# Halving the first batch's attention so that the feed-forward can start earlier

## The chip, the cores and the metric

The kernel runs on one core of a Trainium2 chip. The time is device microseconds of one execution; a figure for a kernel is the median of its runs.

Engines in the profile: PE is the tensor engine's matmuls, PEld its weight loads, DVE the vector engine, ACT the scalar engine, POOL the GpSimd engine, SP the engine that here issues the DMA transposes and the output DMAs. A name such as `po` stands for a tile of the program.

## The reference

Sorted block attention over 4 batches, 8 heads, 768 tokens of 64 values, then a bilinear feed-forward (FFN) over all 3072 tokens.

```python
# q, k, v: (4, 8, 768, 64); sort_net: (4, 8, 8, 8); 8 blocks of 96 tokens
for _ in range(5):                       # P: 8 x 8 per head
    P = exp(P - max(P));  P /= P.sum(-1);  P /= P.sum(-2)
k_sorted = einsum('bhij,bhjcd->bhicd', P, k_b)     # each new block mixes ALL blocks of k
v_sorted = einsum('bhij,bhjcd->bhicd', P, v_b)
scores = scale * q_b @ k_sb.T                      # only inside one block
x = softmax(scores) @ v_sb                         # -> (3072, 512)
out = ((x @ w_a) * (x @ w_b)) @ w_out              # 512 -> 1536 -> 512
```

Sorted k and v need all the tokens of a head, but from the scores on, each block of 96 tokens stands alone. So does each token in the FFN.

## The kernel before

The work is cut into 16 groups `g` of two heads (a "pair"), four pairs to a batch. A batch's FFN needs the x of its four pairs. The kernel does batch 0's attention alone (the "head" of the kernel) and then runs the FFN of batch b with the attention of batch b+1 interleaved. The PE order is fixed by the program; the other engines are ordered by a scheduler. `t` below is one of two halves of a batch's tokens, `m` one of 12 slices of the FFN width.

```python
def to_xT(g, pool, tag):                  # attention result -> transposed x
    xT = xT_of(g // HP)
    nc.sync.dma_start_transpose(out=_ap(xT, ...), in_=st[g, "xp"]...)

def ffn_ab(b, m, t, pool):
    # for w_a, then w_b: four matmuls of 384 columns into pf;
    # ACT copies the first to a_sb, then
    nc.vector.tensor_mul(out=hT[:, m, t * HW:(t + 1) * HW], in0=a_sb, in1=ab[1][:, 0:HW])

def ffn_out(b, c, pool):                  # 128 rows of the output, six times a batch
    po = pool.tile([P, DMODEL], FP32, tag="F", name="po")
    for m in range(KO):
        nc.tensor.matmul(po, lhsT=hT[:, m, c * P:(c + 1) * P], rhs=w_out_sb[:, m, :], ...)
    o_sb = ffp.tile([P, DMODEL], FP32, tag="o_sb", name="o_sb", bufs=3)
    # ACT or DVE copies po to o_sb
    rows = out[b * S:(b + 1) * S, :].rearrange("(p c) n -> c p n", c=NCH)
    nc.sync.dma_start(out=rows[c], in_=o_sb)          # 128 rows, 6 apart
...
for g in range(1, HP):
    stage_q(g, ps0b, "B")                 # q transposes of all four pairs come first
C0(0); C0(1); R0(0); O0(0); to_xT(0, ps0b, "B")       # C: mix, R: scores and v, O: output
C0(2); R0(1); O0(1); to_xT(1, ps0b, "B")
C0(3); R0(2); O0(2); to_xT(2, ps0b, "B")
R0(3); O0(3); to_xT(3, ps0b, "B")
```

The softmax here doesn't subtract the row's maximum and nothing guards it: scores larger than these inputs give would overflow.

## Time and profile before

| | before |
|---|---|
| time, median | 275.3 us at first, 275.81 us over the 4 runs scored with the change |
| span of the profile | 274.4 us |
| PE busy | 238.8 us (87%) |
| first complete FFN (all four matmuls of a group past their waits) | 47.8 us |
| first output matmul (`po`) of batches 0 to 3 | 91.5, 149.2, 207.0, 254.2 us |

The page shows two rows of 40 slices of 6.9 us: the clock granted to PE in tenths, and the mean busy share of the 16 DMA engines in tenths.

```profile
PEclk9999965699999999999999999999999999999999
...
DMA  6999999999993642010110321101011330000132
```

The clock falls to about half in slices 6 to 8 (34 to 55 us).

The next lines are from the page's chain of waits by engine, and from its list of DMAs: count, size of one, median time from issue to landing.

```profile
PE 85%; DMA 7%; POOL 3%; DVE 3%; issue 1%; ACT 0%; POOLq 0%; DVEq 0%; ACTq 0%
...
out_dram<-o_sb SPq DMA_DIRECT2D x24, 256.0 KB, 2.0
...
xT<-xp SPq DMA_TRANSPOSE x16, 2.9
```

PE is 85% of the chain. The same chain in order of time (start, duration, what) shows the head and the first two starts of the output matmuls:

```profile
9.52 8.01 DMA q_102<-in_q_dram
...
17.57 0.85 PE q_ps L131 x9
18.42 2.56 PE mix L145 x40
...
36.64 11.07 DMA xT<-xp
...
47.76 1.76 PE pf L228 x5
...
91.50 0.21 PE po L244
...
149.23 0.22 PE po L244
```

The first mix stands behind the q transposes, and these behind the load that landed at 17.5 us. Later, PE stands behind four DMA transposes of x, one for each pair; the last of them took 11.07 us from issue to landing. From 47.76 us on, everything in this chain up to the last output copy is PE, and a batch takes 57.7 us (149.23 - 91.50).

### The profile page before, as it was taken

Reading aid. Unit: us, or ns where it says so; the run is one execution under the profiler, and the core shown is the slowest. Engines: PE = TensorE matmul, PEld = TensorE weight load, DVE = VectorE, ACT = ScalarE, POOL = GpSimd, SP = SyncE. Lnnn points to the kernel's source line nnn. Section 1 sums busy time; section 2 is a strip of 40 time slices with the busy share of each in tenths; the row PEclk is TensorE's granted clock in tenths of the full one; section 3 lists DMA queues with packets and bytes.
Section 4 is the critical chain, followed back from the end, with each engine's and each line's share of the span. In section 5 each row is a group of like instructions: output and inputs, shape, how many; then the busy total and the mean of one; then the engine's idle time right before and its main releaser. Section 6 shows DMA issues by size and latency. Waiting matters only on the chain.

```text
span 274.4 us, 5477 instructions
## 1 busy us (share of the span) xinstructions
PE 238.8 (87%) x2272; PEld 144.2 (53%) x2280; DVE 122.5 (45%) x268; ACT 98.5 (36%) x194; POOL 48.7 (18%) x67
## 2 busy tenths in 40 slices
PE   0257621999999999999999999999999999999993
PEld 0255510666666545666666446676665455566441
DVE  5836720355555412556554315556644224444111
ACT  2027600446364301644635115354552024333110
POOL 8863349835432000000000000000000000000000
PEclk9999965699999999999999999999999999999999
DMA  6999999999993642010110321101011330000132
GB/s 88 187 202 203 183 183 193 177 185 179 183 176 62 108 122 107 10 29 7 25 31 2 105 102 54 30 2 31 0 32 38 109 113 0 0 2 0 38 117 78
DMA packets 35193, 23.96 MB, mean 87 GB/s; under 512 B 14176, under 2 KB 32096, under 8 KB 35168
## 3 DMA queue, kind: packets, MB, share of 16 engines
q0 software_dynamic: 18864, 14.16, 35.5%
q1 hardware_dynamic: 16304, 9.45, 13.9%
q8 instruction: 18, 0.29, 0.5%
q14 instruction: 7, 0.06, 0.1%
HBM read 28.32 MB, written 6.29 MB: 126 GB/s over the span
## 4 chain that ended last, share of the span: by engine, by line
PE 85%; DMA 7%; POOL 3%; DVE 3%; issue 1%; ACT 0%; POOLq 0%; DVEq 0%; ACTq 0%
PE pf L228 46%; PE po L244 23%; PE mix L145 4%; DMA xT<-xp 4%; PE vs_ps L177 3%; PE o_ps L189 3%; DMA q_102<-in_q_dram 3%; PE sc L166 3%; PE q_ps L131 2%; DVE xp L196 1%; DVE vs_115 L179 1%; DVE rec L193 0%; ACT kT_106 L155 0%; POOL k_77 L78 0%; POOL v_88 L78 0%
## 5 line engine op out<-in xcount | busy, mean ns | idle before, releaser
L228 PE MATMUL pf<-xT,w_a_sb 128*128 128x384 bf16 x384 | 79.9, 330 | 11.3 <-DMA xT<-xp 9.6
L237 DVE TENSOR_TENSOR hT<-a_sb,pf 128x384 bf16<-128x384 bf16 x96 | 53.1, 553 | 78.1 <-PE pf L228 67.9
L228 PE MATMUL pf<-xT,w_b_sb 128*128 128x384 bf16 x384 | 78.8, 328 | 0.0
L236 ACT CAST a_sb<-pf 128x384 bf16<-128x384 f32 x96 | 46.0, 479 | 82.8 <-PE pf L228 51.6
L244 PE MATMUL po<-w_out_sb,hT 128*128 128x512 bf16 x280 | 62.9, 379 | 0.4
L228 PEld LDWEIGHTS <-w_b_sb 128*128 128x128 bf16 x384 | 37.8, 99 | 29.5 <-DMA k_236<-in_k_dram 4.1
L228 PEld LDWEIGHTS <-w_a_sb 128*128 128x128 bf16 x384 | 35.5, 98 | 30.4 <-issue 7.1
L244 PEld LDWEIGHTS <-hT 128*128 128x128 bf16 x288 | 28.0, 98 | 32.8
L250 DVE COPY o_sb<-po 128x512 f32<-128x512 f32 x12 | 8.3, 692 | 43.9 <-PE po L244 43.9
L248 ACT COPY o_sb<-po 128x512 f32<-128x512 f32 x12 | 7.0, 585 | 49.2 <-PE po L244 33.9
L196 DVE TENSOR_TENSOR xp<-o_ps,rec 96x512 bf16<-96x512 f32 x32 | 21.2, 684 | 0.5
L135 DVE COPY qT<-q_ps 128x768 bf16<-128x768 bf16 x16 | 8.8, 551 | 3.4 <-PE q_ps L131 3.4
L155 ACT CAST kT_106<-mix 128x384 bf16<-128x384 f32 x12 | 5.2, 482 | 14.3 <-PE mix L145 14.3
L170 ACT ACTIVATE eT_112<-sc 96x768 bf16<-96x768 f32 x12 | 9.1, 802 | 2.0 <-PE sc L166 1.9
L193 DVE RECIPROCAL rec<-o_ps 96x8 f32<-96x8 f32 x32 | 5.2, 185 | 8.7 <-PE o_ps L189 8.7
L170 ACT ACTIVATE eT_113<-sc 96x768 bf16<-96x768 f32 x10 | 7.5, 803 | 1.2 <-PE sc L166 1.2
L170 ACT ACTIVATE eT_114<-sc 96x768 bf16<-96x768 f32 x10 | 7.5, 802 | 0.9 <-PE sc L166 0.9
L131 PE MATMUL q_ps<-ident,q_81 128*64 128x128 bf16 x12 | 0.9, 313 | 7.8 <-DMA q_81<-in_q_dram 7.8
L155 ACT CAST kT_108<-mix 128x384 bf16<-128x384 f32 x10 | 4.3, 482 | 5.3 <-PE mix L145 5.3
L155 ACT CAST kT_107<-mix 128x384 bf16<-128x384 f32 x10 | 4.3, 482 | 5.1 <-PE mix L145 5.1
L258 POOL TENSOR_TENSOR s_all<-mask,p_col 128x1024 bf16<-128x1024 bf16 x3 | 5.9, 2000 | 0.0
L189 PE MATMUL o_ps<-vs_115,eT_112 96*128 96x65 bf16 x96 | 4.0, 193 | 1.6 <-DVE vs_115 L179 1.6
(205 smaller groups left out, 183.4 us busy)
## 6 DMA issues: line engine op xcount, KB each, us to landing
out_dram<-o_sb SPq DMA_DIRECT2D x24, 256.0 KB, 2.0
w_a_sb<-in_moe_w_a_dram POOLq DMA_DIRECT2D x4, 384.0 KB, 11.4
w_b_sb<-in_moe_w_b_dram POOLq DMA_DIRECT2D x4, 384.0 KB, 12.4
w_out_sb<-in_moe_w_out_dram POOLq DMA_DIRECT2D x3, 512.0 KB, 8.6
xT<-xp SPq DMA_TRANSPOSE x16, 2.9
k_77<-in_k_dram POOLq DMA_DIRECT2D x1, 192.0 KB, 3.5
v_79<-in_v_dram POOLq DMA_DIRECT2D x1, 192.0 KB, 4.6
q_81<-in_q_dram POOLq DMA_DIRECT2D x1, 192.0 KB, 4.9
```

What stands on the lines that cost most here:

```text
L135: nc.vector.tensor_copy(out=qT.rearrange("p i c t -> p c i t"), in_=q_ps.rearrange("p c (i t) -> p c i t", i=NB))
L145: nc.tensor.matmul(mix[e * D:(e + 1) * D, c // 3, c % 3 * P:(c % 3 + 1) * P], lhsT=src2[:, e, c * D:(c + 1) * D], rhs=s_all[:, 2 * g + e], ...
L155: nc.scalar.copy(out=d1, in_=s1)
L166: nc.tensor.matmul(sc[:, e, i * BLK:(i + 1) * BLK], lhsT=kT[e * D:(e + 1) * D, blk * BLK:blk * BLK + P], rhs=qT[e * D:(e + 1) * D, blk], s ...
L170: nc.scalar.activation(out=eT[:, hf, :, 0:HB], in_=sc[0:BLK, :, 0:HB], func=AF.Exp, scale=float(scale))
L189: nc.tensor.matmul(o_ps[:, e, i * (D + 1):(i + 1) * (D + 1)], lhsT=eT[:, hf, e, i * BLK:i * BLK + P], rhs=vs[:, hf * NBH + i, e, 0:D + 1], ...
L196: nc.vector.tensor_tensor(out=_ap(xp, hf * NBH * 2 * D, [[NB * 2 * D, BLK], [D, 2], [2 * D, NBH], [1, D]]), in0=_ap(o_ps, 0, [[1024, BLK], ...
L228: nc.tensor.matmul(pf[:, 0:HW], lhsT=w_sb[:, kc, m * P:(m + 1) * P], rhs=_ap(xT, kc * S + t * 3 * CG, [[KA * S, P], [CG, 3], [BLK, NB], [1 ...
L236: nc.scalar.copy(out=a_sb, in_=pf[:, 0:HW])
L237: nc.vector.tensor_mul(out=hT[:, m, t * HW:(t + 1) * HW], in0=a_sb, in1=ab[1][:, 0:HW])
L244: nc.tensor.matmul(po, lhsT=hT[:, m, c * P:(c + 1) * P], rhs=w_out_sb[:, m, :], start=(m == 0), stop=(m == KO - 1))
L250: nc.vector.tensor_copy(out=o_sb, in_=po)
```

## The change

The intent: let batch 0's FFN start when half of its attention is done. For each pair, only blocks 0 to 3 are scored, normalized and transposed (on PE, with a PSUM copy, instead of by DMA) before the FFN of those blocks starts. Blocks 4 to 7 follow, interleaved with the first FFN half; batch 1's attention is then interleaved with the second half. q is loaded by halves, and the first mix no longer waits for all pairs.

For this, an FFN half must be "four blocks" where it had been "three of six token phases". So the product is written regrouped, and the rows that lie in one output tile change. Core of the diff, with cuts marked by dots and the loop of the head shortened partly into words:

```diff
-    load_pair(0, 0) ... for hp in range(1, HP): load_pair(0, hp)
+    for g in range(HP):
+        load_q_half(g, 0)
+        # k, v of the pair
...
+    def to_xT(g, pool, tag, h, eng):
+        xT, xp = xT_of(g // HP), st[g, "xp"]
+        for i in range(n):
+            nc.tensor.matmul(xt_ps[:, i, :], lhsT=xp[:, i0 + i],
+                             rhs=ident[0:BLK, 0:BLK], is_transpose=True)
+        copy(eng, ...xT..., xt_ps...)
...
-        nc.vector.tensor_mul(out=hT[:, m, t * HW:(t + 1) * HW], in0=a_sb, in1=ab[1][:, 0:HW])
+        nc.vector.tensor_tensor(
+            out=_ap(hTs[b], m * S + t * HW,
+                    [[KO * S, P], [CG, NBH], [NBH * CG, NCH], [1, CG]]),
+            in0=..., in1=_ap(pf, 0, [[512, P], [BLK, NBH], [CG, NCH], [1, CG]]), op=ALU.mult)
...
-        rows = out[b * S:(b + 1) * S, :].rearrange("(p c) n -> c p n", c=NCH)
-        nc.sync.dma_start(out=rows[c], in_=o_sb)
+        nc.sync.dma_start(
+            out=_ap(out, (b * S + t * NBH * BLK + 2 * c) * DMODEL,
+                    [[DMODEL, 2], [NCH * DMODEL, NBH * CG], [1, DMODEL]]),
+            in_=o_sb)
...
+            for g in range(HP + 1):        # head: half 0 only
+                if g < HP:  stage_q(g, ..., 0) if g > 1; mix k, first copy
+                if g > 0:   stage_o(g - 1, ps0, "A", 0)
+                if g < HP:  mix v, first copy; stage_scores(g, ps0, "A", 0)
+                if g > 0:   to_xT(g - 1, ps0b, "B", 0, nc.vector)
+                if g < HP:  stage_v(g, ps0b, "B", 0); second copies of k and v
...
+            second = {0: [(Q1, 0)], 1: [(Q1, 1)], 2: [(S1, 0)], 3: [(V1, 0)], ... 17: [(X1, 3)]}
```

More of the change, by code (lines that the diff above doesn't have):

```diff
@@ L81, in load_pair, with load_q_half @@
         loaded[b * HP + hp] = tiles
-    load_pair(0, 0)
-    make_identity(nc, ident, nomemset=True)
-    for hp in range(1, HP):
-        load_pair(0, hp)
+    HPT = P // 2
+    def load_q_half(g, h):
+        q2 = loaded[g][2]
+        nc.gpsimd.dma_start(
+            out=q2[h * HPT:(h + 1) * HPT],
+            in_=_ap(q, 2 * g * S * D + h * HPT * W, [[W, HPT], [S * D, 2], [1, W]]))
+    make_identity(nc, ident, nomemset=True)
+    for g in range(HP):
+        loaded[g] = [ld.tile([P, 2, W], BF16, tag=n, name=n) for n in ("k2", "v2", "q2")]
+        load_q_half(g, 0)
+        for to, t in zip(loaded[g], (k, v)):
+            nc.gpsimd.dma_start(out=to, in_=_ap(t, 2 * g * S * D, [[W, P], [S * D, 2], [1, W]]))
     mask = const.tile([P, CG], BF16, name="mask")
@@ L95 @@
     NBUF = 3
-    kTs = [const.tile([P, S + PAD], BF16, name=f"kT{n}") for n in range(NBUF)]
-    vTs = [const.tile([P, S + PAD], BF16, name=f"vT{n}") for n in range(NBUF)]
+    NKV = 5
+    HK = HB + PAD
+    kTs = [const.tile([P, 2, HK], BF16, name=f"kT{n}") for n in range(NKV)]
+    vTs = [const.tile([P, 2, HK], BF16, name=f"vT{n}") for n in range(NKV)]
     eTs = [const.tile([BLK, 2, 2, HB + PAD], BF16, name=f"eT{n}") for n in range(NBUF)]
@@ L100 @@
     for t in kTs + vTs:
-        nc.vector.memset(t[:, S:], 0.0)
+        nc.vector.memset(t[:, :, HB:], 0.0)
     for t in eTs:
@@ L124, with copy, blocks, stage_q @@
     st = {}
-    def stage_q(g, pool, tag):
+    def copy(eng, out, in_):
+        if eng is nc.scalar:
+            nc.scalar.copy(out=out, in_=in_)
+        else:
+            eng.tensor_copy(out=out, in_=in_)
+    def blocks(h):
+        return (0, NB) if h is None else (h * NBH, NBH)
+    def stage_q(g, pool, tag, eng, h=None):
         q2 = loaded[g][2]
-        q_ps = pool.tile([P, NCH, P], BF16, tag=tag, name="q_ps")
+        i0, n = blocks(h)
+        p0, np_ = i0 * CG, n * CG
+        q_ps = pool.tile([P, NCH, np_], BF16, tag=tag, name="q_ps")
         for c in range(NCH):
@@ L131, in stage_q, with stage_mix @@
                 nc.tensor.matmul(q_ps[e * D:(e + 1) * D, c, :],
-                                 lhsT=q2[:, e, c * D:(c + 1) * D],
-                                 rhs=ident, is_transpose=True)
-        qT = qtp.tile([P, NB, NCH, CG], BF16, tag="qT", name="qT")
-        nc.vector.tensor_copy(out=qT.rearrange("p i c t -> p c i t"),
-                              in_=q_ps.rearrange("p c (i t) -> p c i t", i=NB))
-        st[g, "qT"] = qT
-    def stage_mix(g, what, pool, tag, engines):
+                                 lhsT=q2[p0:p0 + np_, e, c * D:(c + 1) * D],
+                                 rhs=ident[p0:p0 + np_, p0:p0 + np_], is_transpose=True)
+        if (g, "qT") not in st:
+            st[g, "qT"] = qtp.tile([P, NB, NCH, CG], BF16, tag="qT", name="qT")
+        copy(eng, st[g, "qT"][:, i0:i0 + n].rearrange("p i c t -> p c i t"),
+             q_ps.rearrange("p c (i t) -> p c i t", i=n))
+    def stage_mix(g, what, pool, tag):
         src2 = loaded[g][0 if what == "k" else 1]
-        to = (kTs if what == "k" else vTs)[g % NBUF]
         mix = pool.tile([P, 2, 512], FP32, tag=tag, name="mix")
@@ L145, in stage_mix @@
                 nc.tensor.matmul(
-                    mix[e * D:(e + 1) * D, c // 3, c % 3 * P:(c % 3 + 1) * P],
+                    mix[e * D:(e + 1) * D, c // 4, c % 4 * P:(c % 4 + 1) * P],
                     lhsT=src2[:, e, c * D:(c + 1) * D],
                     rhs=s_all[:, 2 * g + e], start=True, stop=True)
-        for hf, eng in enumerate(engines):
-            n = 2 // len(engines)
-            for u in range(n):
-                d1 = _ap(to, (hf + u) * 3 * CG, [[S + PAD, P], [CG, 3], [BLK, NB], [1, CG]])
-                s1 = _ap(mix, (hf + u) * 512, [[1024, P], [P, 3], [CG, NB], [1, CG]])
-                if eng == "act":
-                    nc.scalar.copy(out=d1, in_=s1)
-                else:
-                    nc.vector.tensor_copy(out=d1, in_=s1)
@@ L159, in stage_scores @@
-    def stage_scores(g, pool, tag):
-        kT, qT, eT = kTs[g % NBUF], st[g, "qT"], eTs[g % NBUF]
-        for hf in range(2):
-            sc = pool.tile([P, 2, 512], FP32, tag=tag, name="sc")
-            for i in range(NBH):
-                for e in range(2):
-                    blk = hf * NBH + i
-                    nc.tensor.matmul(
-                        sc[:, e, i * BLK:(i + 1) * BLK],
-                        lhsT=kT[e * D:(e + 1) * D, blk * BLK:blk * BLK + P],
-                        rhs=qT[e * D:(e + 1) * D, blk], start=True, stop=True)
-            nc.scalar.activation(out=eT[:, hf, :, 0:HB], in_=sc[0:BLK, :, 0:HB],
-                                 func=AF.Exp, scale=float(scale))
@@ L173, in stage_v, with evac_mix @@
-    def stage_v(g, pool, tag):
-        vT, vs = vTs[g % NBUF], vss[g % NBUF]
-        vs_ps = pool.tile([P, NB, 2, D], BF16, tag=tag, name="vs_ps")
-        for i in range(NB):
-            nc.tensor.matmul(vs_ps[:, i], lhsT=vT[:, i * BLK:i * BLK + P],
+        st[g, what] = mix
+    def evac_mix(g, what, eng, h=None):
+        mix, to = st[g, what], (kTs if what == "k" else vTs)[g % NKV]
+        for hf in range(2) if h is None else (h,):
+            copy(eng, _ap(to, hf * HK, [[2 * HK, P], [CG, NCH], [BLK, NBH], [1, CG]]),
+                 _ap(mix, hf * NBH * CG, [[1024, P], [P, NCH], [CG, NBH], [1, CG]]))
@@ new lines, in stage_scores @@
+    def stage_scores(g, pool, tag, h):
+        kT, qT, eT = kTs[g % NKV], st[g, "qT"], eTs[g % NBUF]
+        sc = pool.tile([P, 2, 512], FP32, tag=tag, name="sc")
+        for i in range(NBH):
+            for e in range(2):
+                blk = h * NBH + i
+                nc.tensor.matmul(
+                    sc[:, e, i * BLK:(i + 1) * BLK],
+                    lhsT=kT[e * D:(e + 1) * D, h, i * BLK:i * BLK + P],
+                    rhs=qT[e * D:(e + 1) * D, blk], start=True, stop=True)
+        nc.scalar.activation(out=eT[:, h, :, 0:HB], in_=sc[0:BLK, :, 0:HB],
+                             func=AF.Exp, scale=float(scale))
@@ L178, in stage_v @@
+    def stage_v(g, pool, tag, h=None):
+        vT, vs = vTs[g % NKV], vss[g % NBUF]
+        i0, n = blocks(h)
+        vs_ps = pool.tile([P, n, 2, D], BF16, tag=tag, name="vs_ps")
+        for i in range(n):
+            nc.tensor.matmul(vs_ps[:, i], lhsT=vT[:, (i0 + i) // NBH, (i0 + i) % NBH * BLK:(i0 + i) % NBH * BLK + P],
                              rhs=ident, is_transpose=True)
-        nc.vector.tensor_copy(out=vs[:, :, :, 0:D], in_=vs_ps[0:BLK])
-    def stage_o(g, pool, tag):
+        nc.vector.tensor_copy(out=vs[:, i0:i0 + n, :, 0:D], in_=vs_ps[0:BLK])
@@ L182, in stage_o @@
+    def stage_o(g, pool, tag, h):
         eT, vs = eTs[g % NBUF], vss[g % NBUF]
-        xp = att.tile([BLK, NB, 2, D], BF16, tag="xp", name="xp")
-        rec = att.tile([BLK, 2, 2, NBH], FP32, tag="rec", name="rec")
-        for hf in range(2):
-            o_ps = pool.tile([P, 2, 512], FP32, tag=tag, name="o_ps")
-            for i in range(NBH):
-                for e in range(2):
-                    nc.tensor.matmul(o_ps[:, e, i * (D + 1):(i + 1) * (D + 1)],
-                                     lhsT=eT[:, hf, e, i * BLK:i * BLK + P],
-                                     rhs=vs[:, hf * NBH + i, e, 0:D + 1],
-                                     start=True, stop=True)
-            nc.vector.reciprocal(
-                out=rec[:, hf],
-                in_=_ap(o_ps, D, [[1024, BLK], [512, 2], [D + 1, NBH]]))
-            nc.vector.tensor_tensor(
-                out=_ap(xp, hf * NBH * 2 * D, [[NB * 2 * D, BLK], [D, 2],
-                                               [2 * D, NBH], [1, D]]),
-                in0=_ap(o_ps, 0, [[1024, BLK], [512, 2], [D + 1, NBH], [1, D]]),
-                in1=_ap(rec, hf * 2 * NBH, [[4 * NBH, BLK], [NBH, 2], [1, NBH], [0, D]]),
-                op=ALU.mult)
@@ L202, in stage_o @@
-        st[g, "xp"] = xp
+        if (g, "xp") not in st:
+            st[g, "xp"] = att.tile([BLK, NB, 2, D], BF16, tag="xp", name="xp")
+        xp = st[g, "xp"]
+        rec = att.tile([BLK, 2, NBH], FP32, tag="rec", name="rec")
+        o_ps = pool.tile([P, 2, 512], FP32, tag=tag, name="o_ps")
+        for i in range(NBH):
+            for e in range(2):
+                nc.tensor.matmul(o_ps[:, e, i * (D + 1):(i + 1) * (D + 1)],
+                                 lhsT=eT[:, h, e, i * BLK:i * BLK + P],
+                                 rhs=vs[:, h * NBH + i, e, 0:D + 1],
+                                 start=True, stop=True)
@@ L204 @@
+        nc.vector.reciprocal(
+            out=rec, in_=_ap(o_ps, D, [[1024, BLK], [512, 2], [D + 1, NBH]]))
+        nc.vector.tensor_tensor(
+            out=_ap(xp, h * NBH * 2 * D, [[NB * 2 * D, BLK], [D, 2], [2 * D, NBH], [1, D]]),
+            in0=_ap(o_ps, 0, [[1024, BLK], [512, 2], [D + 1, NBH], [1, D]]),
+            in1=_ap(rec, 0, [[2 * NBH, BLK], [NBH, 2], [1, NBH], [0, D]]),
+            op=ALU.mult)
     xTs = {}
@@ L209, in xT_of, with to_xT_dma @@
         return xTs[b]
-    def to_xT(g, pool, tag):
+    def to_xT(g, pool, tag, h, eng):
+        xT, xp = xT_of(g // HP), st[g, "xp"]
+        i0, n = blocks(h)
+        xt_ps = pool.tile([P, n, BLK], BF16, tag=tag, name="xt_ps")
+        for i in range(n):
+            nc.tensor.matmul(xt_ps[:, i, :], lhsT=xp[:, i0 + i],
+                             rhs=ident[0:BLK, 0:BLK], is_transpose=True)
+        copy(eng, _ap(xT, g % HP * S + i0 * BLK, [[KA * S, P], [1, n * BLK]]),
+             xt_ps.rearrange("p i t -> p (i t)"))
+    def to_xT_dma(g):
         xT = xT_of(g // HP)
@@ L218, with ffn_mm, ffn_a @@
     hTs = {}
-    def ffn_ab(b, m, t, pool):
+    def ffn_mm(b, m, t, w_sb, pool):
+        pf = pool.tile([P, 512], FP32, tag="F", name="pf")
+        for kc in range(KA):
+            nc.tensor.matmul(pf[:, 0:HW], lhsT=w_sb[:, kc, m * P:(m + 1) * P],
+                             rhs=xTs[b][:, kc, t * HW:(t + 1) * HW],
+                             start=(kc == 0), stop=(kc == KA - 1))
+        return pf
+    def ffn_a(b, m, t, pool):
+        pf = ffn_mm(b, m, t, w_a_sb, pool)
+        a_sb = ffp.tile([P, HW], BF16, tag="a_sb", name="a_sb", bufs=4)
+        nc.scalar.copy(out=a_sb, in_=pf[:, 0:HW])
+        st[b, m, t] = a_sb
@@ L221, in ffn_ab, with ffn_b @@
+    def ffn_b(b, m, t, pool):
         if b not in hTs:
             hTs[b] = ffp.tile([P, KO, S], BF16, tag="hT", name="hT")
-        hT, xT = hTs[b], xTs[b]
-        ab = []
-        for w_sb in (w_a_sb, w_b_sb):
-            pf = pool.tile([P, 512], FP32, tag="F", name="pf")
-            for kc in range(KA):
-                nc.tensor.matmul(
-                    pf[:, 0:HW], lhsT=w_sb[:, kc, m * P:(m + 1) * P],
-                    rhs=_ap(xT, kc * S + t * 3 * CG,
-                            [[KA * S, P], [CG, 3], [BLK, NB], [1, CG]]),
-                    start=(kc == 0), stop=(kc == KA - 1))
-            ab.append(pf)
-            if len(ab) == 1:
-                a_sb = ffp.tile([P, HW], BF16, tag="a_sb", name="a_sb", bufs=4)
-                nc.scalar.copy(out=a_sb, in_=pf[:, 0:HW])
@@ L237, in ffn_ab @@
-        nc.vector.tensor_mul(out=hT[:, m, t * HW:(t + 1) * HW], in0=a_sb,
-                             in1=ab[1][:, 0:HW])
-    def ffn_out(b, c, pool):
+        pf = ffn_mm(b, m, t, w_b_sb, pool)
+        nc.vector.tensor_tensor(
+            out=_ap(hTs[b], m * S + t * HW,
+                    [[KO * S, P], [CG, NBH], [NBH * CG, NCH], [1, CG]]),
+            in0=st[b, m, t].rearrange("p (i c s) -> p i c s", i=NBH, c=NCH),
+            in1=_ap(pf, 0, [[512, P], [BLK, NBH], [CG, NCH], [1, CG]]),
+            op=ALU.mult)
@@ L241, in ffn_out @@
+    def ffn_out(b, t, c, pool):
         hT = hTs[b]
+        c0 = t * HW + c * P
         po = pool.tile([P, DMODEL], FP32, tag="F", name="po")
         for m in range(KO):
-            nc.tensor.matmul(po, lhsT=hT[:, m, c * P:(c + 1) * P], rhs=w_out_sb[:, m, :],
+            nc.tensor.matmul(po, lhsT=hT[:, m, c0:c0 + P], rhs=w_out_sb[:, m, :],
                              start=(m == 0), stop=(m == KO - 1))
         o_sb = ffp.tile([P, DMODEL], FP32, tag="o_sb", name="o_sb", bufs=3)
-        if c % 2 == 0:
-            nc.scalar.copy(out=o_sb, in_=po)
-        else:
-            nc.vector.tensor_copy(out=o_sb, in_=po)
@@ L251, in ffn_out @@
-        rows = out[b * S:(b + 1) * S, :].rearrange("(p c) n -> c p n", c=NCH)
-        nc.sync.dma_start(out=rows[c], in_=o_sb)
+        copy(nc.scalar if c % 2 == 0 else nc.vector, o_sb, po)
+        nc.sync.dma_start(
+            out=_ap(out, (b * S + t * NBH * BLK + 2 * c) * DMODEL,
+                    [[DMODEL, 2], [NCH * DMODEL, NBH * CG], [1, DMODEL]]),
+            in_=o_sb)
     s_all = const.tile([P, BH, NB, CG], BF16, name="s_all")
@@ L267 @@
                 tc.tile_pool(name="ps0b", bufs=2, space=PSUM) as ps0b:
-            stage_q(0, ps0, "A")
             rsum = const.tile([BH, NB], FP32, name="rsum")
@@ L282 @@
                                      in1=_ap(csum, 0, [[NB, BH], [0, NB], [1, NB]]))
-            nc.vector.tensor_copy(out=p_rep, in_=_ap(p_fin, 0, [[NB * NB, BH], [NB, NB],
-                                                                [1, NB], [0, CG]]))
+            for h, eng in enumerate((nc.vector, nc.scalar)):
+                copy(eng, p_rep[:, h * NBH:(h + 1) * NBH],
+                     _ap(p_fin, h * NBH * NB, [[NB * NB, BH], [NB, NBH], [1, NB], [0, CG]]))
+            stage_q(0, ps0b, "B", nc.scalar, 0)
+            stage_q(1, ps0b, "B", nc.scalar, 0)
             pc_ps = ps0.tile([P, NB, BH], FP32, tag="A", name="pc_ps")
@@ L292 @@
             nc.vector.tensor_copy(out=p_col, in_=pc_ps)
-            for c in range(4):
+            load_ab(0)
+            for g in range(HP):
+                load_q_half(g, 1)
+            for c in range(1, 4):
                 load_ab(c)
@@ L300 @@
                 load_out(c)
-            def C0(g):
-                stage_mix(g, "k", ps0, "A", ("act",))
-                stage_mix(g, "v", ps0, "A", ("act", "dve"))
-            def R0(g):
-                stage_scores(g, ps0, "A")
-                stage_v(g, ps0b, "B")
-            def O0(g):
-                stage_o(g, ps0, "A")
-            for g in range(1, HP):
-                stage_q(g, ps0b, "B")
-            C0(0); C0(1); R0(0); O0(0); to_xT(0, ps0b, "B")
-            C0(2); R0(1); O0(1); to_xT(1, ps0b, "B")
-            C0(3); R0(2); O0(2); to_xT(2, ps0b, "B")
-            R0(3); O0(3); to_xT(3, ps0b, "B")
+            for g in range(HP + 1):
+                if g < HP:
+                    if g > 1:
+                        stage_q(g, ps0b, "B", nc.scalar, 0)
+                    stage_mix(g, "k", ps0, "A")
+                    evac_mix(g, "k", nc.scalar, 0)
+                if g > 0:
+                    stage_o(g - 1, ps0, "A", 0)
+                if g < HP:
+                    stage_mix(g, "v", ps0, "A")
+                    evac_mix(g, "v", nc.scalar, 0)
+                    stage_scores(g, ps0, "A", 0)
+                if g > 0:
+                    to_xT(g - 1, ps0b, "B", 0, nc.vector)
+                if g < HP:
+                    stage_v(g, ps0b, "B", 0)
+                    evac_mix(g, "k", nc.scalar, 1)
+                    evac_mix(g, "v", nc.vector, 1)
         with tc.tile_pool(name="psA", bufs=2, space=PSUM) as psA, \
@@ L323, with Q1, S1, V1 @@
                 tc.tile_pool(name="psF", bufs=3, space=PSUM) as psF:
+            def Q1(g):
+                stage_q(g, psB, "B", nc.vector, 1)
+            def S1(g):
+                stage_scores(g, psA, "A", 1)
+            def V1(g):
+                stage_v(g, psB, "B", 1)
+            def O1(g):
+                stage_o(g, psA, "A", 1)
+            def X1(g):
+                to_xT(g, psB, "B", 1, nc.vector)
+            def C(g):
+                stage_q(g, psB, "B", nc.vector)
+                stage_mix(g, "k", psA, "A")
+                evac_mix(g, "k", nc.scalar)
+                stage_mix(g, "v", psA, "A")
+                evac_mix(g, "v", nc.vector)
+            def R(g):
+                stage_scores(g, psA, "A", 0)
+                stage_scores(g, psA, "A", 1)
+                stage_v(g, psB, "B")
+            def O(g):
+                stage_o(g, psA, "A", 0)
+                stage_o(g, psA, "A", 1)
+                to_xT_dma(g)
+            second = {0: [(Q1, 0)], 1: [(Q1, 1)], 2: [(S1, 0)], 3: [(V1, 0)], 4: [(S1, 1)],
+                      5: [(O1, 0), (V1, 1)], 6: [(Q1, 2)], 7: [(X1, 0)], 8: [(S1, 2), (O1, 1)],
+                      9: [(V1, 2)], 10: [(Q1, 3)], 11: [(X1, 1)], 12: [(S1, 3), (O1, 2)],
+                      13: [(V1, 3)], 14: [(X1, 2)], 15: [(O1, 3)], 17: [(X1, 3)]}
             for b in range(B):
@@ L327 @@
                         load_pair(b + 2, hp)
-                units = []
-                if b + 1 < B:
-                    for g in range((b + 1) * HP, (b + 2) * HP):
-                        def c_(g=g):
-                            stage_q(g, psB, "B")
-                            stage_mix(g, "k", psA, "A", ("act",))
-                            stage_mix(g, "v", psA, "A", ("dve", "act"))
-                        def r_(g=g):
-                            stage_scores(g, psA, "A")
-                            stage_v(g, psB, "B")
-                        def o_(g=g):
-                            stage_o(g, psA, "A")
-                        def x_(g=g):
-                            to_xT(g, psB, "B")
-                        units += [c_, r_, o_, x_]
@@ L343 @@
-                steps = [lambda m=m, t=t, b=b: ffn_ab(b, m, t, psF)
-                         for m in range(KO) for t in range(2)]
-                outs = [lambda c=c, b=b: ffn_out(b, c, psF) for c in range(NCH)]
-                steps += outs
-                n, done = len(steps), 0
+                order = ([(m, t) for t in range(2) for m in range(KO)] if b == 0 else
+                         [(m, t) for m in range(KO) for t in range(2)])
+                steps = []
+                for m, t in order:
+                    steps.append(lambda m=m, t=t, b=b: ffn_a(b, m, t, psF))
+                    steps.append(lambda m=m, t=t, b=b: ffn_b(b, m, t, psF))
@@ new lines @@
+                for t in range(2):
+                    for c in range(3):
+                        steps.append(lambda t=t, c=c, b=b: ffn_out(b, t, c, psF))
+                n = len(steps)
+                after = {s: [] for s in range(n)}
+                first = 0
+                if b == 0:
+                    for s, u in second.items():
+                        after[s] += u
+                    first = 24
+                if b + 1 < B:
+                    units = [(f, g) for g in range((b + 1) * HP, (b + 2) * HP) for f in (C, R, O)]
+                    for k_, u in enumerate(units):
+                        after[first + k_ * (n - 4 - first) // len(units)].append(u)
@@ L348 @@
                 for s, step in enumerate(steps):
                     step()
-                    want = -(-(s + 1) * len(units) // (n - 2))
-                    while done < min(want, len(units)):
-                        units[done]()
-                        done += 1
+                    for f, g in after[s]:
+                        f(g)
 _INS = ['q', 'k', 'v', 'sort_net', 'moe_w_a', 'moe_w_b', 'moe_w_out']
```

## The prediction

> **What bounds the kernel now.** The tensor engine: PE is 85% of the chain of waits, and from 50 us on the table by windows shows it busy almost without a gap. So time = start of the first feed-forward (FFN) matmul + PE work after it. From the chain: batch 0 runs 47.8 to 107.6 us, batches 1 and 2 take 57.7 us each, the last (no attention beside it) 47.0, the tail 4.4. Attention beside the FFN thus costs PE 10.7 us a batch.
>
> The avoidable part is the head. PE transposes q of all four head pairs first, so the first mix waits for the last load (17.5 us), though the sort weights were ready at about 12.9. Attention of batch 0 ends at 36.6; then PE waits for four DMA transposes of x: 11.1 us in the chain, "DMA xT<-xp". Meanwhile the granted clock falls to 0.50 (36 to about 53 us). The Trainium skill, "TensorE: Matmul & The Clock Gate", Part 1, says that some 3.4 us of idling halves the clock until PE has been busy as long again; the trace agrees: batch 0 took 59.8 us against 57.7, 2.1 lost.
>
> **What the change does.**
> 1. The first mix waits only for its own pair and the sort weights: 17.6 -> 13 us.
> 2. Only block half 0 stands before the FFN. ACT per pair: four copies (0.48 us, 0.38 back to back) and one exp (0.75): 2.3 us. DVE, half-size copies estimated from full ones: 0.19 + 0.69 + 0.56 + 0.42 + 0.36 = 2.2 us. Neither bounds alone; the order does (exp, second k copy, q copy, next k copy, scores; three PSUM buffers for four live tiles): I estimate 3.1 us a pair. First exp ends near 15.8, the fourth near 25.1, then output, normalize, transpose, copy: first FFN matmul at **27.5 us** (25 to 31) instead of 47.8.
> 3. Batch 0's x transposes go to PE: no 11 us wait, little cold clock.
> 4. Half 1 moves under the first FFN half: q 0.35 + scores 0.23 + v 0.28 + output 0.26 + transpose 0.25, with switches 1.45 us a pair (estimate from full-size pieces): +5.8 us PE.
> 5. Batch 1's attention is squeezed into FFN half 1. DVE then has about 5.8 us of work per 6.6 us of PE: I allow 1.5 us of stalls.
> 6. From batch 1 on: same PE work; one of three k/v copies per pair moves from ACT to DVE, which has room (58% busy in 120 to 140 us): nothing. The regrouped FFN product stays 0.55 us.
>
> Sum: 27.5 + (47.0 + 10.7 + 5.8 + 1.5 + 0.5 cold) + 115.4 + 47.0 + 4.4 = 259.8 us of span; timed runs are about 1 us longer: **261 us**, 256 to 268. Faster by over 2%: 0.94; within 2%: 0.05; slower: 0.01.
>
> **What would show it.** First FFN matmul before 31 us, no wait of PE for a transpose of batch 0; mixes starting near 13 us; granted clock not at 0.5 for more than one slice after 28 us; batch 0's FFN lasting 63 to 67 us; batches 1 to 3 unchanged within 0.5 us.
>
> **What would make it wrong.** The head is a chain across PE, ACT and DVE: at 4 us a pair the FFN starts at 31. The first weight chunk must land (I expect 20 us, at 0.97 us per 192 KB) and later ones keep ahead; a second q half landing late stops the in-order PE. Batch 1's loads and its sort-weight spread on POOL must come before about 48 us. If DVE backs up in FFN half 1, PE stalls more.

## More of the kernel before

The DMA engines are full until about 80 us and mostly idle after 100.

An output DMA landed 2.0 us after its issue.

The view of the output tile `o_sb` (calls, min/median/max ns; last line: landing) and two slices of 1 us of the table by windows in the last output phase (columns: window, busy time of PE, PEld, DVE, ACT, POOL with counts, clock, DMA share, GB/s) are worth keeping for later:

```profile
L252 SPq DMA_DIRECT2D out_dram<-o_sb x24: 332/332/354, 94.7 to 270.6; - x24
L248 ACT COPY o_sb<-po x12: 585/585/586, 94.1 to 267.2; 128x512 f32<-128x512 f32 x12
L250 DVE COPY o_sb<-po x12: 691/692/692, 97.2 to 269.8; 128x512 f32<-128x512 f32 x12
...
DMA to landing us min/median/max: 2.0/2.0/3.7
```

```profile
core 0: us, PE busy (x) PEld busy (x) DVE busy (x) ACT busy (x) POOL busy (x), PEclk, DMA share, GB/s
266.00:267.00 1.00, 1.00 (x7) 0.41 (x6) 0.00 (x0) 0.00 (x0) 0.00 (x0) 1.00 0.70 262
267.00:268.00 1.00, 1.00 (x6) 0.48 (x5) 0.00 (x0) 0.58 (x1) 0.00 (x0) 1.00 0.00 0
```

An output DMA takes the 16 engines to 0.70 for one slice, and they are idle in the next. Nobody waits for it.

## The result, and the profile after

302.56 us (301.83 to 304.6, 4 runs) against 275.81 us (274.44 to 277.43, 4 runs): slower by a factor of 1.0979, 95% interval 1.0896 to 1.1063.

| | before | after |
|---|---|---|
| span | 274.4 us | 300.4 us |
| first complete FFN group | 47.8 us | 29.0 us |
| first `po` matmul of batches 0 to 3 | 91.5, 149.2, 207.0, 254.2 | 79.8, 145.1, 208.3, 262.5 |
| from one to the next | 57.7, 57.7, 47.3 | 65.3, 63.2, 54.3 |
| last first-`po` to the end | 20.2 | 37.9 |

The head did what was predicted: FFN at 29.0 us instead of 47.8, and batch 0 was 11.7 us ahead at its first output matmul. Then 7.6, 5.5 and 7.0 us were lost from one first `po` to the next, 20.1 in all, and another 17.7 after the last. The same parts of the page as before:

```profile
PEclk9999799999999779999999799999996899999855
...
DMA  6999999999961114101111170110111100001111
```

The clock is no longer halved at 40 us, but dips once a batch and at the end. The DMA row now shows a low, long plateau, mostly at 1 tenth.

```profile
PE 66%; DMA 22%; ACT 2%; DVE 2%; POOL 1%; issue 1%; ACTq 0%; POOLq 0%
...
out_dram<-o_sb SPq DMA_DIRECT2D x24, 256.0 KB
```

PE fell to 66% of the chain, DMA rose to 22%, 17% of it output DMAs. The list of DMAs gives no landing time for them any more. The chain in order of time, around the first FFN and the first output phase:

```profile
28.62 0.37 DVE xT L144
...
29.03 0.81 PE pf L255 x4
...
79.83 0.22 PE po L282
...
80.11 7.51 PE po L282 x34
...
87.64 0.59 ACT o_sb L142
...
88.25 13.56 DMA out_dram<-o_sb
...
145.08 0.21 PE po L282
```

There is no wait for an x transpose by DMA. But behind the third output copy stands an output DMA of 13.56 us. The view of `o_sb`, to be held against the one of before, and a window in the tail, when all other work was done:

```profile
L286 SPq DMA_DIRECT2D out_dram<-o_sb x24: 507/512/1334, 83.7 to 284.5; - x24
L142 ACT COPY o_sb<-po x16: 586/586/587, 82.5 to 283.9; 128x512 f32<-128x512 f32 x16
L144 DVE COPY o_sb<-po x8: 691/692/693, 85.1 to 278.8; 128x512 f32<-128x512 f32 x8
...
who waited for it (us, times):
  ACT o_sb L142: 50.5, 8
  DVE o_sb L144: 31.9, 3
  PE pf L255: 13.7, 5
```

```profile
core 0: us, PE busy (x) PEld busy (x) DVE busy (x) ACT busy (x) POOL busy (x), PEclk, DMA share, GB/s
286.00:296.00 10.00, 0.00 (x0) 0.00 (x0) 0.00 (x0) 0.00 (x0) 0.00 (x0) 0.50 0.13 51
```

Copies into an output tile waited 82.4 us in sum for output DMAs that had not finished; before, none did. PE in turn waited 13.7 us for these copies, 4.0 to 5.1 after each of the first three batches, and after each wait it worked at a clock of 0.50 for a while: 12.8 us of work in all (102.6 to 108.4, 167.2 to 169.8 and 230.3 to 234.7 us), which at full clock would take about half, an estimate of 6.4 us lost. Together that is about the 20.1 us. In the tail the DMA engines together were busy for a share of 0.13, as much as two of 16, at 51 GB/s, where one slice of before shows 0.70 at 262 GB/s.

### The profile page after: what moved, and what is told of

It reads as the page before. It is cut to its first block, busy times and chain, and to the rows that moved or that the text cites. A ratio compares the mean times of both kernels' runs of the same rounds, so it can differ in the third digit from the quotient of the medians.

```text
span 300.4 us, 5638 instructions
## 1 busy us (share of the span) xinstructions
PE 248.9 (83%) x2352; PEld 147.8 (49%) x2360; DVE 126.7 (42%) x292; ACT 98.0 (33%) x191; POOL 50.7 (17%) x71
## 4 chain that ended last, share of the span: by engine, by line
PE 66%; DMA 22%; ACT 2%; DVE 2%; POOL 1%; issue 1%; ACTq 0%; POOLq 0%
PE pf L255 43%; DMA out_dram<-o_sb 17%; PE po L282 10%; PE mix L169 3%; PE o_ps L212 3%; PE vs_ps L199 3%; DMA q_82<-in_q_dram 3%; PE q_ps L156 2%; PE sc L187 2%; DMA k_86<-in_k_dram 2%; ACT o_sb L142 2%; PE xt_ps L237 0%; DVE hT L270 0%; DVE xT L144 0%; ACT kT_109 L142 0%
## 5 line engine op out<-in xcount | busy, mean ns | idle before, releaser
L255 PE MATMUL pf<-xT,w_a_sb 128*128 128x384 bf16 x384 | 82.1, 338 | 12.8 <-ACT o_sb L142 12.4
L255 PE MATMUL pf<-xT,w_b_sb 128*128 128x384 bf16 x384 | 81.3, 336 | 1.3 <-DVE o_sb L144 1.3
L255 PEld LDWEIGHTS <-w_a_sb 128*128 128x128 bf16 x384 | 36.9, 100 | 37.7 <-issue 16.7
L255 PEld LDWEIGHTS <-w_b_sb 128*128 128x128 bf16 x384 | 36.9, 100 | 25.8 <-issue 4.6
L142 ACT COPY o_sb<-po 128x512 f32<-128x512 f32 x16 | 9.4, 586 | 80.4 <-DMA out_dram<-o_sb 50.5
L144 DVE COPY o_sb<-po 128x512 f32<-128x512 f32 x8 | 5.5, 692 | 59.4 <-DMA out_dram<-o_sb 31.9
L144 DVE COPY qT<-q_ps 128x768 bf16<-128x768 bf16 (+1 forms) x16 | 8.0, 502 | 3.3 <-PE q_ps L156 3.3
L201 DVE COPY vs_119<-vs_ps 96x512 bf16<-96x512 bf16 (+1 forms) x8 | 4.4, 551 | 2.9 <-PE vs_ps L199 2.8
L201 DVE COPY vs_121<-vs_ps 96x1024 bf16<-96x1024 bf16 (+1 forms) x6 | 3.6, 595 | 4.0 <-PE vs_ps L199 4.0
L212 PEld LDWEIGHTS <-eT_116 96*128 96x128 bf16 x96 | 4.2, 100 | 1.6 <-ACT eT_116 L191 0.5
L201 DVE COPY vs_120<-vs_ps 96x1024 bf16<-96x1024 bf16 (+1 forms) x6 | 3.5, 590 | 2.7 <-PE vs_ps L199 2.7
```

The costliest lines, as they stand in the source:

```text
L142: nc.scalar.copy(out=out, in_=in_)
L144: eng.tensor_copy(out=out, in_=in_)
L201: nc.vector.tensor_copy(out=vs[:, i0:i0 + n, :, 0:D], in_=vs_ps[0:BLK])
L212: nc.tensor.matmul(o_ps[:, e, i * (D + 1):(i + 1) * (D + 1)], lhsT=eT[:, h, e, i * BLK:i * BLK + P], rhs=vs[:, h * NBH + i, e, 0:D + 1], s ...
L255: nc.tensor.matmul(pf[:, 0:HW], lhsT=w_sb[:, kc, m * P:(m + 1) * P], rhs=xTs[b][:, kc, t * HW:(t + 1) * HW], start=(kc == 0), stop=(kc == ...
```

## The experiments

**Theory A.** One output DMA is spread over only two of the 16 DMA engines, because the slowest dimension of its destination pattern has become 2. The Trainium skill, "DMA: Bandwidth & Descriptors", section "Why a DMA increments its semaphore by 16 and not by 1", paragraph "How many engines (k)", states that the slowest dimension of size above 1 of each pattern is looked at, and the largest number up to 16 that divides both sizes is the number of engines. Here the SBUF side has 128 and the destination 2, hence 2; before, it was 128 and 128, hence 16. With the page's figure of about 27 GiB/s per engine (its "Specifications"; 29 GB/s) the estimate is 4.5 us for 256 KB on two engines. The window above shows 51 GB/s, 25.6 per engine if there are two, or 5.1 us. A batch's six output tiles are 2.6 us apart (12 `po` matmuls each, 0.22 us a matmul in the chain of before), and there are three buffers: the queue of DMAs grows until the copies stop, then PE has no free PSUM buffer and stops too.

**Theory B.** The destination rows of one DMA are now pairs of neighbours, which could be written slowly; or the new interleaving, not the DMA, starves the copies.

### Mending the DMA alone: e1_two64

```diff
-        nc.sync.dma_start(out=_ap(out, ..., [[DMODEL, 2], [NCH * DMODEL, NBH * CG], [1, DMODEL]]), in_=o_sb)
+        for u in range(2):
+            nc.sync.dma_start(
+                out=_ap(out, (b * S + t * NBH * BLK + 2 * c + u) * DMODEL,
+                        [[NCH * DMODEL, NBH * CG], [1, DMODEL]]),
+                in_=o_sb[u * 64:(u + 1) * 64])
```

> The changed kernel with each 128-row output DMA issued as two of 64 rows, so that the slowest dimension of the destination pattern is 64 instead of 2; same rows, same 2 KB pieces, nothing else changed. Theory A (a DMA is spread over as many of the 16 DMA engines as divide the slowest dimension of its pattern, here 2): landing about 2 us instead of 5 us apart, no PE wait for an output tile, time about 262 us (258 to 266). Theory B (the row pairs that lie side by side in memory are written slowly, or the new interleaving starves the output copies): no or little gain, 295 to 303 us.

Measured: 264.42 us (263.5 to 266.4), ratio to before 0.9602 (0.9551 to 0.9653). This is what theory A expected. The chain runs through its output phases without a stop; these lines are batches 0 and 1:

```profile
81.11 15.54 PE po L282 x72
96.65 0.65 PE pf L255 x4
...
138.83 15.54 PE po L282 x72
154.37 0.65 PE pf L255 x4
```

```profile
L287 SPq DMA_DIRECT2D out_dram<-o_sb x48: 466/566/1032, 84.3 to 260.0; - x48
...
DMA to landing us min/median/max: 2.2/2.3/2.8
```

The output phase of 72 matmuls takes 15.54 us and is followed at once by the next FFN. An output DMA of 64 rows lands after 2.3 us. (The split is not free: the packet records in the kept traces show 154 ns for a row of 2 KB here, in the median of all output rows, and 84 in the changed kernel.) Interleaving and head are those of the changed kernel, so theory B's starving falls. The 38.1 us (302.56 - 264.42) are the output DMA's, with the waits and the slow clock that it brought. A single DMA no longer holds neighbouring rows here, so the other half of theory B is still open.

### More buffers instead: e4_bufs8

```diff
-        o_sb = ffp.tile([P, DMODEL], FP32, tag="o_sb", name="o_sb", bufs=3)
+        o_sb = ffp.tile([P, DMODEL], FP32, tag="o_sb", name="o_sb", bufs=8)
```

> The changed kernel with 8 instead of 3 output tiles, DMA unchanged. Theory A: the six slow DMAs of a batch need about 31 us of two engines, less than a batch's 58, so with buffers enough the waits inside batches 0 to 2 go (about 7 us each) and only the end stays long, because the last six still take 31 us: about 281 us (277 to 286). Theory B (interleaving of copies): no change, 300 to 304.

Measured: 282.29 us (280.71 to 283.97), ratio 1.0242 (1.0185 to 1.0298), as theory A expected. No copy waits for an output DMA any more, and the first `po` of batch 3 comes at 243.7 us, as in e1_two64 (243.3) and not at 262.5. From there to the end it is still 37.8 us, against 20.2. So of the 36.9 us by which the spans of the changed kernel and e1_two64 differ (300.4 - 263.5), about 19 were lost inside batches 0 to 2 (PE waits and the slow clock after them), which buffers can hide, and about 18 lie in the last six outputs, which they can't. Its page shows the plateau of the last batch at about 50 GB/s with PE done:

```profile
DMA  6999998999992119111021185310111110001111
GB/s 82 183 202 203 202 201 127 185 202 196 160 178 56 54 51 72 58 23 30 1 51 51 54 68 51 42 29 2 40 51 54 51 51 9 0 30 51 51 51 40
```

### The cause put into the kernel before: b_outer2 and b_outer16

The kernel before, with the rows of an output tile permuted so that the same 128 rows are written by a pattern of n x 128/n rows (n = 2 below).

```diff
-        nc.vector.tensor_mul(out=hT[:, m, t * HW:(t + 1) * HW], in0=a_sb, in1=ab[1][:, 0:HW])
+        nc.vector.tensor_mul(
+            out=_ap(hT, m * S + t * HW, [[KO * S, P], [P, 3], [1, P // 2], [P // 2, 2]]),   # 2: n
+            in0=a_sb.rearrange("p (c h l) -> p c h l", c=3, l=2),
+            in1=ab[1][:, 0:HW].rearrange("p (c h l) -> p c h l", c=3, l=2))
...
-        nc.sync.dma_start(out=rows[c], in_=o_sb)
+        nc.sync.dma_start(
+            out=_ap(out, (b * S + c) * DMODEL,
+                    [[NCH * DMODEL, 2], [2 * NCH * DMODEL, P // 2], [1, DMODEL]]),
+            in_=o_sb)
```

> The kernel before with nothing changed but the order of the 128 rows of an output tile (even ones first), so that its output DMA writes the same rows by a pattern of 2 x 64 rows. Theory A: outputs 5 us apart, the tensor engine waits at the end of each batch, +35 to +45 us: 310 to 320 us; DMA share near 2/16 in the tail. Theory B (interleaving of the changed kernel): stays 274 to 277.

> Control for b_outer2: the same edit of the kernel before, with a pattern of 16 x 8 rows. Theory A: all 16 engines, landing about 2 us, 274 to 278 us. A rival by which any destination pattern of three dimensions, or the permuted writes of the feed-forward product, is slow: 300 us or more.

Measured: 364.07 us (ratio 1.3193) and 326.68 us (ratio 1.1851). Both missed what theory A expected of them: the control was meant to stay at 275. Its profile shows why. The product `hT` took 1907 ns where it had taken 553, because its two-byte results are now written 16 bytes or more apart, and DVE bounds the FFN (with results in runs of 16 neighbours, in b_outlayout below, the product takes 552 ns; here it is 33% and 39% of the two chains). My edit had a cost of its own; as a control it is spoiled, as a pair the two still speak, since the product costs the same in both (1910 and 1907 ns): 37.4 us between a pattern of 2 x 64 and one of 16 x 8.

### The same without the spoiled product: b_outlayout

I took instead the change's own output side, whose product takes 0.55 us, into the kernel before.

```diff
-                    rhs=_ap(xT, kc * S + t * 3 * CG, [[KA * S, P], [CG, 3], [BLK, NB], [1, CG]]),
+                    rhs=xT[:, kc, t * HW:(t + 1) * HW],
...
# product and output DMA as in the change; schedule, attention, DMA transposes as before
```

> The kernel before with only the output side of the change: feed-forward halves by blocks, its regrouped product, and the 2 x 64 row output pattern; schedule, attention and x by DMA as before. b_outer2 and b_outer16 were confounded by slow permuted product writes (1.9 us); this product took 0.55 us in the changed kernel. Theory A (two DMA engines per output DMA): the changed kernel lost 38 us against its two-DMA mending, so here too +35 to +42: 310 to 318 us. Rival (it takes the new interleaving to be slow): 274 to 280.

Measured: 315.61 us (314.22 to 316.51), ratio 1.1439 (1.1389 to 1.1489). That is +39.9 us on the kernel before (275.67 in these rounds), next to +38.1 us between the mended and the unmended change. The product took 552 ns. So the loss belongs to the output side, in either schedule. The tail, from the issue of the last output DMA to the end, shows the low DMA share of the change, here in the schedule of before:

```profile
298.30:314.60 16.30, 0.00 (x0) 0.00 (x0) 0.00 (x0) 0.00 (x0) 0.00 (x0) 0.50 0.12 45
```

### A dose: b_outer4 and b_outer8

The edit of b_outer2 with 4 x 32 and 8 x 16 rows; one run each, state unknown.

> The same edit as b_outer2 and b_outer16 with a pattern of 4 x 32 rows. Theory A (k engines share an output DMA, about 25 GB/s each, plus a fixed 2.2 us read from b_outer16): landing about 4.8 us, DMAs no longer queue (2.6 us of transfer, 2.6 us apart), no wait for output tiles worth naming, 327 to 333 us, far from 364. If instead two slow engines of the 16 were the matter: as b_outer2.

> The same with 8 x 16 rows. Theory A: landing about 3.5 us, 326 to 329 us.

Measured: 329.09 us, within its range, and 321.18 us, below it. Times beside b_outer16's 326.68 are blurred by the slow product (1874, 1822 and 1907 ns), so I read the DMA share while outputs are on their way, in the last output phase. One line of the windows each, for patterns of 2, 4, 8 and 16 (the last for the fullest single slice, since an output needs only about 1 us):

```profile
335.00:345.00 10.00, 5.20 (x25) 2.16 (x22) 0.69 (x1) 0.58 (x1) 0.00 (x0) 1.00 0.13 51
```

```profile
308.00:318.00 10.00, 7.90 (x36) 3.42 (x35) 1.39 (x2) 1.17 (x2) 0.00 (x0) 1.00 0.26 80
```

```profile
303.00:313.00 10.00, 9.56 (x44) 4.13 (x43) 0.99 (x2) 1.17 (x2) 0.00 (x0) 1.00 0.42 103
```

```profile
315.00:316.00 1.00, 1.00 (x6) 0.49 (x5) 0.00 (x0) 0.36 (x1) 0.00 (x0) 1.00 0.91 231
```

The shares, 0.13, 0.26, 0.42 and 0.91, stand beside 2/16, 4/16, 8/16 and 16/16. Those of 8 and 16 include some idle time. The packet records in the kept traces, which have the start and duration of every row of 2 KB, settle the count without an average: in the last output phase the number of rows on their way at a time was most often 2, 4, 8 and 15 or 16 for these patterns, 2 in the changed kernel (for 90% of the time in which any was) and 16 in the kernel before. And a row was not written more slowly: 84 ns in the median for all four patterns and for the change, 86 before. With the pattern of 4, output copies still waited 31.2 us for DMAs in sum (92.7 us with 2, none with 8, 2.2 with 16): at 80 GB/s, 256 KB take 3.3 us, which is more than the 2.6 us between outputs. I had expected no such waits with 4. The rate doesn't grow in step with the engines, though (51, 80 and 103 GB/s for 2, 4 and 8): the mean time of a row in the last output phase rises from 87 to 105 and 133 ns, for a reason that stays open. The landing times that I had forecast for 4 and 8 the profile did not give. All four write the same rows in the same 2 KB pieces, none of them neighbours within a DMA, and only the grouping differs. So the rest of theory B falls too: slow writing of neighbouring rows isn't needed for the effect, and with the neighbouring rows of the changed kernel the share and rate are no worse (0.13 and 51 GB/s in both).

### What the halving itself is worth: e5, e9, e10

The mended change takes 264.4 us, which is 11 us better than before. Is that the halves, or only the x transposes on PE?

e5_before_xpe: the kernel before, with batch 0's x transposed on PE, each right behind its pair's output.

```diff
+    def to_xT_pe(g, pool, tag):
+        xt_ps = pool.tile([P, NB, BLK], BF16, tag=tag, name="xt_ps")
+        for i in range(NB):
+            nc.tensor.matmul(xt_ps[:, i, :], lhsT=xp[:, i], rhs=ident[0:BLK, 0:BLK], is_transpose=True)
+        nc.vector.tensor_copy(out=...xT..., in_=...xt_ps...)
-            C0(0); C0(1); R0(0); O0(0); to_xT(0, ps0b, "B")
+            C0(0); C0(1); R0(0); O0(0); to_xT_pe(0, ps0b, "B")      # and so for 1 to 3
```

> The kernel before with only the x transposes of batch 0 on PE (with a DVE copy), no halves. If the 11 us wait for DMA transposes and the cold clock after it are the whole avoidable cost: first feed-forward matmul near 38 us, batch 0 in about 58 us, 262 to 266 us in all, as fast as the mended change (264.4). If halving the first batch is what pays: 268 us or more.

Measured: 272.25 us, ratio 0.9876: a miss. The first FFN came at 44.9 us, not at 38. The program fixes the order of PE, and every transpose waits there for the normalization just before it; the head ran at the slow clock besides (16 score matmuls in 0.82 us at 38.7 us, in 0.51 at 50.1). Waits of PE from 18 to 46 us (sum in us, times, longest):

```profile
PE xt_ps L221 <- DVE xp L196: 4.0, 8, 0.8
PE o_ps L189 <- DVE vs L179: 3.1, 4, 0.8
```

e9_before_xpe_late moves each transpose behind the next pair's scores and v:

```diff
-            C0(2); R0(1); O0(1); to_xT_pe(1, ps0b, "B")
+            C0(2); R0(1); to_xT_pe(0, ps0b, "B"); O0(1)
...
```

> e5 with each PE transpose of x moved behind the next pair's scores and v, so that the in-order tensor engine does not wait for the normalization (e5's first feed-forward matmul came at 44.9 us, with PE waits of about 1.7 us a pair). If that placement is what e5 lost: first feed-forward matmul at 37 to 40 us, 262 to 267 us. If not: 270 or more.

Measured: 265.87 us, ratio 0.961 (0.9569 to 0.9652). First FFN at 36.8 us. The waits for the normalization went from eight to two. The two lines below fall by 3.7 us in sum; the rest of the 8.1 us by which the FFN starts earlier goes mostly with the clock, which was 0.50 from 27.0 us on in e5 (PE worked for 12.2 us at that clock before its FFN) and here only from 37.3 us on:

```profile
PE o_ps L189 <- DVE vs L179: 2.1, 4, 0.8
PE xt_ps L221 <- DVE xp L196: 1.3, 2, 0.8
```

e10_whole_interleaved takes the change's order of the head for whole blocks, loads q first, and lets ACT copy q:

```diff
+            for g in range(HP + 1):
+                if g < HP:  stage_q(g, ..., nc.scalar) if g > 0; stage_mix(g, "k", ...)
+                if g > 0:   stage_o(g - 1, ps0, "A")
+                if g < HP:  stage_mix(g, "v", ...); stage_scores(g, ps0, "A")
+                if g > 0:   to_xT_pe(g - 1, ps0b, "B")
+                if g < HP:  stage_v(g, ps0b, "B")
```

> The kernel before with x of batch 0 on PE, q loaded first, q copies of the head on ACT, and the changed kernel's interleaving of the head loop, but whole blocks: nothing moved under the feed-forward. If halves add more feed-forward time (67.6 us for batch 0 in the mended change against 57.7) than they save in the head: first feed-forward matmul by 36 us and 258 to 263 us, faster than the mended change (264.4). If halves pay: 266 or more.

Measured: 266.79 us, ratio 0.9651 (0.9611 to 0.9692); first FFN at 36.8 us: a miss, since I had expected 36 us at most and 258 to 263. Its head was no shorter than e9's.

So with whole blocks (0.961, 0.965) and with halves (0.960) the ratio to before is the same within the intervals; I can't tell which is faster, and the rules by which e5, e7 and e10 would each say that halves pay were too sharp for that. The sum explains it. With halves the FFN starts 6.7 us earlier (30.15 against 36.8 us), but batch 0 then takes until its first `po` 51.0 us (81.11 - 30.15) instead of 45.5 (82.33 - 36.80), because half of the attention now runs inside it. Only 1.2 us of lead are left at that point.

### The other part undone: e6 and e7

e6_two64_xdma is the mended change with batch 0's x by DMA transposes again, in halves.

```diff
-                    to_xT(g - 1, ps0b, "B", 0, nc.vector)
+                    to_xT_dma_half(g - 1, 0)
...
-                to_xT(g, psB, "B", 1, nc.vector)
+                to_xT_dma_half(g, 1)
```

> The mended change (two 64-row output DMAs) with batch 0's x brought back to DMA transposes, half by half. If the transposes still queue behind the loads (up to 11 us in the kernel before), the first feed-forward matmul moves from 29 to 35 to 42 us and the time to 270 to 278 us. If halving alone had removed that cost: 264 to 267.

Measured: 273.15 us, ratio 0.9916 (0.9857 to 0.9974), so most of the gain is gone. The first FFN matmul came at 25.3 us, but its group of four then waited for three transposes and was complete only at 32.8 us, and two more waits came at the second FFN half. The five waits of PE:

```profile
PE pf L262 <- DMA xT<-xp: 10.6, 5, 3.1
```

The x transposes of that kernel, early and late ones together, landed after 4.5 us in the median and 9.7 at most. The time is as expected; the mechanism was more spread out than a first FFN matmul at 35 to 42 us.

e7_before_xpe_early is e5 plus an early first mix, q loaded first and q copies on ACT.

```diff
-        for name, t in (("k2", k), ("v2", v), ("q2", q)):
+        for name, t in (("q2", q), ("k2", k), ("v2", v)):
...
-            for g in range(1, HP):
-                stage_q(g, ps0b, "B")
-            C0(0); C0(1); R0(0); ...
+            C0(0); stage_q(1, ps0b, "B", nc.scalar); C0(1); R0(0); ...   # q 2 and 3 likewise
```

> e5 and three small edits of the head: q first among the loads, the first mixes no longer behind the q transposes of all pairs, q copies of the head on ACT. No halves, no work moved under the feed-forward. First mix near 13 us, first feed-forward matmul at 32 to 35, 257 to 261 us: faster than the mended change, if keeping batch 0 whole costs no more head time than halving costs feed-forward time. If halves pay: 263 or more.

Measured: 270.16 us, ratio 0.9796 (0.9757 to 0.9835): a miss, for e5's reason. The first mix started at 13.0 us, but the PE transposes still stood right behind the outputs, and the first FFN came at 41.4 us. Neither e5 nor e7 told halves from whole blocks; e9 was made for that. Whether a better order of a whole-block head would beat halves is left open.

## Why the prediction was wrong

It said 261 us, faster by over 2% at 0.94. The kernel took 302.56. Point by point:

- "First FFN matmul at 27.5 us (25 to 31)": 29.0 us. Right, including the mixes near 13 us (12.99) and no PE wait for a DMA transpose of batch 0. The 29.0 has some luck in it: the same head took until 30.15 us in e1 and 30.25 in e4, where 12 mix matmuls at 23.6 us still took 0.85 us, and 0.53 in the changed kernel.
- "+5.8 us PE" for half 1, "1.5 us of stalls", "0.5 cold", together 65.5 us for batch 0: 66.5 us in the mended kernel (30.15 to 96.65). Right.
- "115.4 + 47.0 + 4.4" for the rest: 115.4 + 46.8 + 4.7 in the mended kernel. Right there; in the changed kernel, from one first `po` to the next it was 65.3 and 63.2 us instead of 57.7. The check "batches 1 to 3 unchanged within 0.5 us" failed, and with it the check of the clock (0.50 after every stall and in the last two slices).
- The failed step is point 6: "From batch 1 on: same PE work [...] nothing." It costed the PE work, the k/v copies and the product, and never the output DMA, which stands in the diff as a rewritten pattern. The same rows in the same 2 KB pieces were in effect taken for the same transfer. It is not: two rows on their way at a time instead of 16, and 38.1 us in the changed schedule, 39.9 in the old one, all by the grouping of its rows. This hit the terms "115.4 + 47.0" (20.1 us between the first `po` of batches 0 to 3) and "4.4" (17.7 us after the last).
- "What would make it wrong" named the head, the weights, the loads and DVE. None of them made the loss. The sum of the mended kernel came to 263.5 us of span against 259.8 predicted, an error of 3.7, most of it the head's 30.15 us.

The skill's paragraph on the number of engines would have given the 2 before the run, had I looked it up for the changed DMA, as I had looked up the clock. What the page on the clock, "TensorE: Matmul & The Clock Gate", Part 1, says of idling held again: after the last matmul, at 278.0 us, the changed kernel's clock fell within 282 to 283 us and its tail was granted 0.50 throughout (286 to 296 us). But idling is not needed: in e5 the clock fell at 27.0 us without a PE wait over 0.8 us since 18 us.

## What to carry to other kernels

When a change rewrites the access pattern of a DMA, cost the DMA anew, even if bytes, rows and pieces stay the same: look at the outermost dimension of both sides, and make it a multiple of 16 (16, 64 and 128 kept about 16 engines busy here), for instance by splitting the DMA as in e1; swapping the dimensions was not tried. In the trace, look at the DMA share while only that transfer runs: 0.13 is two engines of 16. And when a change bundles several ideas, try the cheapest one alone: here moving four pairs of transposes off the DMA engines, at the right place in the PE order, gave what the whole restructuring gave.

## What the Trainium skill lacked or had wrong

- "DMA: Bandwidth & Descriptors", "How many engines (k)": agrees with these runs (shares of 0.13, 0.26, 0.42 and 0.91 for 2, 4, 8 and 16). It lacks a worked example of a 128-row store whose rows are grouped as 2 x 64, and its cost: 38.1 us of 302.56 here, where an output that had landed 2.0 us after its issue now needs 5.1 us of transfer alone (256 KB at 51 GB/s), one behind the other.
- The same page, "Specifications": about 27 GiB/s (29 GB/s) per engine; these runs show 51 GB/s for two engines, 25.6 each, for stores of 2 KB rows, 80 GB/s for four, 20 each, and 103 GB/s for eight, 13 each.
- "SBUF — State Buffer" gives 16-byte cache lines and says that each access that crosses to a new line pays. A DVE product of 384 bf16 elements from PSUM whose results were written 16 to 128 bytes apart took 1822 to 1910 ns against 553 ns contiguous, 3.3 to 3.5 times as long; I found no figure for two-byte results of a product there; those on the DVE pages are for four-byte words.
- I found no page that gives the delay of a DMA transpose that runs beside loads: 11.1 us at most in the kernel before, 2.9 in the median.
- "TensorE: Matmul & The Clock Gate", Part 1, gives no busy share below which the clock falls without an idle window. In these runs it fell after 3.4 us in which PE was busy for 2.0 us (e5, 23.6 to 27.0 us), 1.7 (e7, 22.4 to 25.8) and 1.6 (before, 32.4 to 35.8), and stayed full in the 3.4 us before each of these, with 2.2, 2.1 and 2.4 us.
